# Moving transposes of k with q to the DMA queue from chunk 8, of x from chunk 12, in a new program order

## The chip, the cores and the metric

One core of a Trainium2 chip. The metric is the device time of the program in microseconds (us); most executions agree within a per cent, and a median of several is quoted. All comparisons are with runs of the kernel before in the same session. The sessions of the experiments were on different chips (2, 12, 0, 14 and 7), and the median of the kernel before moved from 186.6 to 187.6 us between sessions, so ratios are worth more here than medians. A ratio is the mean time of one kernel's fast runs over the mean of the other's fast runs of the same rounds, so it is not quite the ratio of the medians beside it.

## The reference

A gated linear recurrence over 4 batches x 8 heads x 768 steps, head size 48, whose output is the input of an MLP with the gate h cos(h):

```python
for t in range(S):
    state = alpha[:, :, t, :, None] * state + einsum('bhd,bhe->bhde', k[:, :, t], v[:, :, t])
    y[:, :, t] = einsum('bhd,bhde->bhe', q[:, :, t], state)
x = y.transpose(0, 2, 1, 3).reshape(3072, 384)
h = x @ w_in                      # 384 -> 2048
out = (h * cos(h)) @ w_out        # 2048 -> 384
```

The kernel cuts the 3072 tokens into 24 chunks of 128. Within a chunk the recurrence is turned into matrix products: scores of scaled q with scaled k, masked, times v, plus q times the state so far.

## The kernel before

Every chunk needs its scaled k and q (the tile `kqb`) transposed for the scores, and its output y transposed into x for the MLP. Each transpose exists in two forms, chosen by the chunk's number: eight (or three) matmuls against the identity on TensorE into a PSUM bank plus a copy by VectorE, or one transposing DMA that SyncE issues.

```python
TD = 13
QB = 6
XD = 13
...
def transposes(j):
    ...
    if j >= TD:
        t = work.tile([C, 2 * NP, C], BF, tag="qkT", bufs=QB)
        nc.sync.dma_start_transpose(out=t, in_=kqb[:, j % 3].rearrange("s i h d -> s (i h d)"))
        qkT_t[j] = t.rearrange("r b s -> r (b s)")
        return
    t = ps.tile([C, 2 * NP * C], BF, tag="g")
    ...     # eight nc.tensor.transpose; ev_transposes() copies the bank out on VectorE

def x_transposes(j):
    if j >= XD:
        x = work.tile([C, 3, C], BF, tag="xT", bufs=3)
        nc.sync.dma_start_transpose(out=x, in_=y_t.pop(j))
        ...
```

All loads of alpha, k, q, v and the weights are DMAs that SyncE issues too, one after the other in program order; ScalarE issues the stores of the result and a small copy of the decays. The order of all work is a hand-written string of units, each a letter and a chunk (or a pair of chunks):

```python
ORDER = ("a0 l0 C0 a2 l1 k0 C1 q0 E0 K0 E1 Q0 w8 T0 t0 v0 k2 N0 ...")
# a k q v: loads;  l C E: decays (log, sums, exps);  K Q b: GpSimd scales k, q, casts v
# T t: transposes of kqb and their copy;  A m: scores, mask;  S u: state;  Y y: outputs and their copy
# D B: transposes of x and their copy;  F G: first MLP product, two halves;  f_ g_ p Q_: gate
# V W: second MLP product, two halves;  e: result out;  w: warm-up matmuls
```

In the traces each engine works through its part of this order in turn, a unit that waits holds the later ones of its engine, and a DMA that waits for its input on SyncE holds the loads behind it. In the kernel before, SyncE had come to the next two transposes of x at 135.7 us; it issued them at 137.7 and 140.9, each when VectorE's copy of its y had ended, and the load of k behind them at 142.3.

## Time and profile before

| | before |
|---|---|
| median time, first session | 186.19 us (186.08 to 189.03) |
| span of the profiled execution | 185.2 us |
| TensorE busy | 173.1 us, 93% |
| first MLP matmul / end of the last one | 26.11 / 181.72 us |
| stops of TensorE in between | 2.4 us |
| transposing DMAs of kqb / of x | 11 / 11 |

A stop is counted from the starts of successive matmuls: where the distance exceeds the usual one of that kind of matmul by over 0.15 us, the excess is a stop. What remains between the first MLP matmul and the end of the last one is called work below. The first line below, from the page of the kernel before, is the mean busy share of the 16 DMA engines in tenths, in 40 slices of 4.6 us; the second is the queue of SyncE's DMAs, with packets, MB and the share of the engines' time:

```profile
DMA  6999999999999999998999889985994964222012
q1 hardware_dynamic: 108304, 29.14, 76.5%
```

Until about 125 us, the DMA engines are as full as TensorE is.

### The profile page before, as it was taken

Reading aid. Unit: us, or ns where it says so; the run is one execution under the profiler, and the core shown is the slowest. Engines: PE = TensorE matmul, PEld = TensorE weight load, DVE = VectorE, ACT = ScalarE, POOL = GpSimd, SP = SyncE. Lnnn points to the kernel's source line nnn. Section 1 sums busy time; section 2 is a strip of 40 time slices with the busy share of each in tenths; the row PEclk is TensorE's granted clock in tenths of the full one; section 3 lists DMA queues with packets and bytes.
Section 4 is the critical chain, followed back from the end, with each engine's and each line's share of the span. In section 5 each row is a group of like instructions: output and inputs, shape, how many; then the busy total and the mean of one; then the engine's idle time right before and its main releaser. Section 6 shows DMA issues by size and latency. Waiting matters only on the chain.

```text
span 185.2 us, 5549 instructions
## 1 busy us (share of the span) xinstructions
PE 173.1 (93%) x2326; PEld 135.7 (73%) x2329; DVE 132.1 (71%) x183; ACT 121.4 (66%) x140; POOL 75.8 (41%) x106
## 2 busy tenths in 40 slices
PE   0898888999999999999989999999999999999992
PEld 0555567986688878779848798698767989698761
DVE  6477799999677875986793897916792877655620
ACT  3855589698568679779578777776468726353521
POOL 3373730419345472927942812684032753100000
PEclk9999999999999999999999999999999999999999
DMA  6999999999999999998999889985994964222012
GB/s 147 261 261 229 360 386 333 373 187 211 211 226 157 237 188 204 198 213 166 221 146 250 165 150 191 198 186 100 188 183 89 203 146 103 64 66 65 4 42 85
DMA packets 113080, 34.24 MB, mean 185 GB/s; under 512 B 106400, under 2 KB 111520, under 8 KB 113056
## 3 DMA queue, kind: packets, MB, share of 16 engines
q1 hardware_dynamic: 108304, 29.14, 76.5%
q10 hardware_dynamic: 4752, 4.76, 8.1%
q8 instruction: 18, 0.29, 0.7%
q14 instruction: 6, 0.05, 0.1%
HBM read 25.17 MB, written 4.72 MB: 161 GB/s over the span
## 4 chain that ended last, share of the span: by engine, by line
PE 83%; DVE 8%; DMA 5%; ACT 1%; issue 1%; DVEq 0%
PE o_new L488 33%; PE t L466 32%; DMA t<-kqb 3%; PE t L371 3%; DVE t L380 3%; PE t L428 2%; DMA a_new<-in_alpha_dram 2%; PE t L396 2%; DVE t L357 2%; PE w_new L504 2%; PE cum_new L227 2%; PE t L344 2%; PE t L425 2%; PE t L449 1%; DVE w L160 1%; PE t L315 1%
## 5 line engine op out<-in xcount | busy, mean ns | idle before, releaser
L466 PE MATMUL t<-x,w 128*128 128x128 bf16 x1152 | 70.3, 219 | 0.0
L488 PE MATMUL o_new<-w,g_new 128*128 128x384 bf16 x384 | 68.0, 326 | 0.0
L480 DVE TENSOR_TENSOR g_new<-t,c_sb 128x1024 bf16<-128x1024 f32 x48 | 57.6, 1218 | 13.0 <-ACT c_sb L474 12.9
L466 PEld LDWEIGHTS <-w 128*128 128x128 bf16 x1152 | 65.7, 98 | 1.1
L474 ACT ACTIVATE c_sb<-t,halfpi 128x1024 bf16<-128x1024 f32 x48 | 52.7, 1112 | 21.1 <-PE t L466 18.9
L488 PEld LDWEIGHTS <-g_new 128*128 128x128 bf16 x384 | 35.6, 98 | 20.9
L380 DVE TENSOR_TENSOR t<-t,mask_f 128x1024 bf16<-128x1024 f32 x24 | 29.0, 1218 | 2.2 <-PE t L371 2.2
L410 POOL TENSOR_TENSOR ub<-sc,Em 128x384 bf16<-128x384 f32 x16 | 13.3, 829 | 36.2 <-DVE sc L408 35.9
L279 POOL TENSOR_TENSOR kqb<-raw_new,cpx 128x384 bf16<-128x384 f32 x18 | 21.3, 1188 | 15.4 <-DMA raw_new<-in_q_dram 9.1
L493 ACT ACTIVATE o_sb<-o_new 128x384 f32<-128x384 f32 x24 | 11.7, 488 | 18.0 <-PE o_new L488 18.0
L263 POOL TENSOR_TENSOR kqb<-raw_new,icp_new 128x384 bf16<-128x384 f32 x18 | 18.0, 1001 | 5.3 <-DMA raw_new<-in_k_dram 3.9
L435 DVE CAST t<-t 128x384 bf16<-128x384 f32 x24 | 13.3, 553 | 7.5 <-PE t L428 7.4
L288 POOL CAST vpb<-raw_new 128x384 bf16<-128x384 f32 x20 | 9.9, 504 | 14.0 <-DMA raw_new<-in_v_dram 6.5
L408 DVE TENSOR_TENSOR sc<-t,ub 128x384 f32<-128x384 f32 x16 | 8.9, 554 | 7.3 <-PE t L396 7.2
L238 ACT ACTIVATE icp_new<-cum_new 128x768 f32<-128x768 f32 x12 | 9.7, 809 | 5.5 <-PE cum_new L227 3.4
L474 ACT ACT_TABLE_LOAD x8 | 10.3, 1283 | 2.9 <-DVE t L435 0.6
L183 ACT ACT_TABLE_LOAD x8 | 10.3, 1283 | 2.0 <-ACT o_sb L493 1.2
L428 PE MATMUL t<-vpb,t 128*128 128x48 bf16 x192 | 11.3, 183 | 0.3 <-DVE t L357 0.3
L428 PEld LDWEIGHTS <-t 128*128 128x128 bf16 x192 | 9.6, 96 | 1.1 <-DVE t L357 0.6
L425 PE MATMUL t<-ub,t 128*128 128x96 bf16 x80 | 9.7, 204 | 0.4 <-DVE t L357 0.4
L371 PE MATMUL t<-t 48*128 48x128 bf16 x192 | 8.2, 218 | 0.7 <-DMA t<-kqb 0.7
L357 DVE COPY t<-t 128x512 bf16<-128x512 bf16 x12 | 7.7, 684 | 1.2 <-PE t L331 1.2
(68 smaller groups left out, 146.6 us busy)
## 6 DMA issues: line engine op xcount, KB each, us to landing
out_dram<-o_sb ACTq DMA_DIRECT2D x24, 192.0 KB, 3.1
raw_new<-in_v_dram SPq DMA_DIRECT2D x20, 192.0 KB, 4.7
a_new<-in_alpha_dram SPq DMA_DIRECT2D x18, 192.0 KB, 4.9
raw_new<-in_k_dram SPq DMA_DIRECT2D x18, 192.0 KB, 4.5
raw_new<-in_q_dram SPq DMA_DIRECT2D x18, 192.0 KB, 4.7
wf<-in_moe_w_in_dram SPq DMA_DIRECT2D x4, 768.0 KB, 8.8
wf<-in_moe_w_out_dram SPq DMA_DIRECT2D x4, 768.0 KB, 9.7
a_new<-in_alpha_dram SPq DMA_DIRECT2D x3, 384.0 KB, 4.6
```

The source lines that it names most:

```text
L263: nc.gpsimd.tensor_tensor(out=khb[:, j % 3, :, 0:D], in0=k_t.pop(j), in1=icp.rearrange("s (h d) -> s h d", h=H), op=ALU.mult)
L279: eng.tensor_tensor(out=qhb[:, j % 3, :, 0:D].rearrange("s (p a) d -> s p a d", a=2), in0=q_t.pop(j).rearrange("s (p a) d -> s p a d", a=2 ...
L371: nc.tensor.matmul(t[:, ACOL[h] * C : (ACOL[h] + 1) * C], qkT_t[j][base : base + D, p * C : (p + 1) * C], qkT_t[j][base : base + D, (NP + ...
L380: nc.vector.tensor_tensor(out=t.rearrange("s (h t) -> s h t", h=H), in0=A_ps.pop(j).rearrange("s (h t) -> s h t", h=H), in1=mask_f.unsquee ...
L410: eng.tensor_tensor(out=ub[:, us(j), :, 0:96].rearrange("r p (a e) -> r p a e", a=2), in0=sc.rearrange("r p (a e) -> r p a e", a=2), in1=E ...
L425: nc.tensor.matmul(t[:, p * 96 : (p + 1) * 96], qT[:, (NP + p) * C : (NP + p + 1) * C], ub[:, us(j - 1), p], start=True, stop=False, skip_ ...
L428: nc.tensor.matmul(t[:, h * D : (h + 1) * D], A_t[j][:, ACOL[h] * C : (ACOL[h] + 1) * C], vpb[:, j % 3, h], start=first, stop=True, skip_g ...
L435: nc.vector.tensor_copy(out=t, in_=y_ps.pop(j)[:, 0:HD])
L466: nc.tensor.matmul(t[:, f], w1[:, kk, ft * C : (ft + 1) * C], x_t[j][:, kk], start=(kk == 0), stop=(kk == 2))
L474: nc.scalar.activation(out=c_sb, in_=h_ps[j, half], func=AF.Sin, bias=halfpi, scale=1.0)
L480: nc.vector.tensor_tensor(out=g_new, in0=h_ps.pop((j, half)), in1=c_t.pop((j, half)), op=ALU.mult)
L488: nc.tensor.matmul(o_ps[j][:, 0:DM], g[:, f], w2[:, half * HF + f], start=(f == 0 and half == 0), stop=(f == HF - 1 and half == 1))
```

## The change

Intent: TensorE is the bound, so take five chunks' transposes of k with q, and one of x, off it and off VectorE, and put them on DMA, in an order meant to suit.

```diff
-    TD = 13
+    TD = 8
     QB = 6
-    XD = 13
+    XD = 12
     ...
     ORDER = (
-        "a0 l0 C0 a2 l1 k0 C1 q0 E0 K0 E1 Q0 w8 T0 t0 v0 k2 N0 b0 n0 N1 n1 v2 M0 M1 T1 t1 o0 w5 S0 o1 E_0 a4 "
+        "a0 k0 l0 C0 E0 a2 K0 w13 T0 l1 N0 q0 Q0 t0 v0 C1 q2 b0 M0 n0 E_0 o0 k2 a4 E1 K2 T1 t1 w6 S0 u0 A0 l2 "
     ...  # the whole string is new; nothing else is
```

## The prediction

> **What bounds the kernel now.** I read the page's busy shares first, then the chain of work that ended last, then TensorE's instructions in order of time, the costliest groups, and last the DMA issues.
>
> ```profile
> PE 173.1 (93%) x2326; PEld 135.7 (73%) x2329; DVE 132.1 (71%) x183; ACT 121.4 (66%) x140; POOL 75.8 (41%) x106
> ...
> PE   0898888999999999999989999999999999999992
> ...
> PE 83%; DVE 8%; DMA 5%; ACT 1%; issue 1%; DVEq 0%
> ```
>
> The page's chain has its shares by engine in that last line. From the costliest groups (mean ns of one after the busy time, then idle time before it), what the change removes:
>
> ```profile
> L360 DVE COPY t<-t 128x1024 bf16<-128x1024 bf16 x7 | 4.8, 689 | 3.5 <-PE t L344 3.4
> L454 DVE COPY x<-t 128x384 bf16<-128x384 bf16 x13 | 4.6, 352 | 2.7 <-PE t L449 2.7
> ...
> L449 PE MATMUL t<-ident_bf,t 128*128 128x128 bf16 x39 | 4.3, 220 | 0.6 <-DVE t L435 0.5
> L344 PE MATMUL t<-ident_bf,kqb 128*128 128x128 bf16 x56 | 4.3, 219 | 0.0
> ```
>
> TensorE is nearly always occupied, no other engine passes 71%, and 83% of the chain lies on TensorE. A mean of 219 ns for a transpose is not its cost, because matmuls overlap. The chain in order of time gives the cost, the time that a unit adds:
>
> ```profile
> 34.40 0.17 PE t L449 x3
> 34.56 2.68 PE t L466 x48
> ...
> 45.33 0.45 PE t L344 x8
> ...
> 89.69 6.04 DMA t<-kqb
> ...
> 176.52 5.21 PE o_new L488 x32
> 181.76 0.49 ACT o_sb L493
> ```
>
> So half a chunk's first MLP product (24 matmuls) costs 1.34 us, half of the second (8) 1.30, a chunk's transposes of k with q (8) 0.45, its transposes of x (3) 0.17. The last matmul ends at 181.76 of a 185.2 us span; the 3.5 us after it are one copy and one store. The MLP alone is 48 x 1.34 + 48 x 1.30 = 126.7 us.
>
> TensorE's instructions in order of time, and ScalarE's casts of the weights, show where it still stops:
>
> ```profile
> 23.26 0.63 ACT L158 ACTIVATE w<-wf 128x512 bf16<-128x512 f32 x1 [1.86 <-DMA wf<-in_moe_w_in_dram]
> ```
>
> ```profile
> 26.11 1.50 PE L466 MATMUL t<-x,w 128*128 128x128 bf16 x24
> ...
> 28.64 0.34 PE L449 MATMUL t<-ident_bf,t 128*128 128x128 bf16 x3 [0.32 <-DVE t L435]
> ...
> 32.52 0.20 PE L425 MATMUL t<-ub,t 128*128 128x96 bf16 x1 [0.42 <-DVE t L357]
> ...
> 95.77 0.40 PE L371 MATMUL t<-t 48*128 48x128 bf16 x8 [0.69 <-DMA t<-kqb]
> ```
>
> Three stages follow. Up to 26.1 us nothing of the MLP runs: its weights are still on the way (the first quarter of the first matrix lands at 23.24 us, the second at 25.27, each 2.03 us apart in a stream with no gap). From 26.1 to 33 us TensorE works with stops. After that it is full, except for 0.69 us at 95 us. From the first MLP matmul to the last one are 181.76 - 26.11 = 155.65 us. From the pitch of successive matmuls against each kind's usual pitch I count stops of 0.45, 0.58, 0.28, 0.17 and 0.76 us, together 2.24 us; the other 153.4 us are work.
>
> [...] The trace [...] shows 219 ns a transpose, of which only 56 ns keep TensorE: it is the smaller number that a removed transpose is worth. [...] Two of them issued one behind the other land 0.75 us apart here (99.17 and 99.92 us), 256 KB in 0.75 us or 350 GB/s[...]; but issue to landing is 3.6 us in the median and 6.0 at worst, since they stand behind loads. [...] I add up pitches and not the 93%.
>
> **The change part by part.**
>
> Transposes of k with q: chunks 8 to 12 go from TensorE to DMA (16 chunks in place of 11). TensorE loses 5 x 0.45 = 2.25 us. VectorE loses 5 copies of 0.69 = 3.4 us. DMA gains 5 x about 0.9 us.
>
> Transposes of x: chunk 12 alone. TensorE loses 0.17 us, VectorE 0.35, DMA gains some 0.4 (the distance of two such landings, 117.11 and 117.53).
>
> Order, before the first MLP matmul: the same twelve loads stand ahead of the weights in both programs, so I expect the first two quarters at about 23.2 and 25.3 us again. The new program starts on the first half of the MLP, of which the quarter that is loaded second is needed first: 25.3 plus a cast of 0.6 gives 25.95 to 26.05 us. No gain here, though VectorE's work ahead of it now leaves more gaps: the start is bound by DMA.
>
> Order, after it: the same MLP units, scores, outputs and states; one permutation (0.33 us) now lies before the first MLP matmul, two warm-up matmuls (2 x 0.217) lie after it. The work from the first MLP matmul on is 153.4 - 2.25 - 0.17 - 0.33 + 0.43 = 151.1 us.
>
> ScalarE: counting the switches between logarithm and sine in program order gives 14 table loads, not 16: 2 x 1.28 = 2.6 us less on an engine with a third of its time idle; worth nothing by itself.
>
> Stops: the transposes, states, outputs and x share one PSUM bank (tag g, one buffer), so each must be copied out before the next may start. Summing TensorE's durations between neighbours in the order, against the copy that has to fit in between, I find two places that don't fit in the program before (0.38 and 0.05 us short, the first where the 0.45 us stop is) and none in the new one, which also has six users of that bank fewer. The 0.45, 0.28 and most of the 0.58 should go.
>
> New stops: in the last three chunks the order leaves 4.8, 4.1 and 3.9 us of other TensorE work between an output's matmuls and the first use of its transposed x, where it left 10.4, 5.7 and 5.3 us. What must fit is a copy (0.55) and a transpose DMA (2.3 / 3.1 / 4.3 us minimum, median, maximum): 2.9 to 4.9 us. At the median it fits, at the worst it is 1 us short each. I allow 0.5 us there, 0.5 for transposes behind loads around chunks 8 to 18 (the scores of chunks 8, 9 and 16 to 18 stand right behind their transposes in the order, though SyncE may issue these earlier), and 0.5 for the start from 26 to 42 us, where weights land one after another up to 39.6 us and the new order consumes them just behind. Together 1.5 us.
>
> Sum: 26.0 + 151.1 + 1.5 = 178.6 us for the last matmul, plus 3.5 = 182.1 us of span, 3.1 below 185.2. In times: 186.2 - 3.1, about 183.1 us.
>
> **The rivals.**
>
> One: the transposes on DMA turn into waits. For it: the only long stop past 33 us is one (0.69 us), it ends a 6.04 us flight, and SyncE issues loads and transposes in one order, so a transpose that waits for k or q holds back all loads behind it. Chunks 8 to 12 fall where loads still stream (loads land about every 1.0 us until 92 us). Against it: ten of eleven such transposes made TensorE wait for nothing, and GpSimd, which makes their inputs, is busy 41%. If every one of the five cost 0.7 us, 3.5 us would be lost: about 185.6 to 186.6 us.
>
> Two: the order has removed more than I see. If the stops shrink to 0.5 us in all, and the start gains half a microsecond because loads are arranged better, the span is 25.5 + 151.1 + 0.5 + 3.5 = 180.6 us, a time of 181.6.
>
> Three: the relief of VectorE and ScalarE is what counts. Against it: VectorE is 71% busy, ends few of TensorE's waits after 33 us, and its longest waits are for ScalarE and TensorE. Then only TensorE's 2.3 us would be gained by accident; a kernel with the old order and the new limits would tell.
>
> **Range and chances.** TensorE's own sum, -2.3 us, is sure to some 0.3 us. The stops may be 0.5 to 4 us (2.2 now), the start 25.5 to 26.8 us. So 183.1 us, with 181.4 to 185.3 for eight in ten. Faster by over 2% is below 182.5 us; that needs stops under 0.9 us, which I give 0.32. Within 2%: 0.65. Slower by over 2% would need over 7 us of waits: 0.03.
>
> **What would show it.** In the new profile: 16 transposes of kqb on TensorE (chunks 6 and 7; the group of L344 falls from x56 to x16) and 16 transpose DMAs of kqb, 12 of x; the first MLP matmul at 26 us, behind a weight's cast; stops of TensorE after it of about 1.5 us; the last matmul at 178 to 179 us with one copy and one store after it. I would be wrong if TensorE showed waits for kqb's or x's transposes of over 2 us in sum, if the first MLP matmul moved by over a microsecond, or if the weights of the second MLP product, which land last, hold up its first use at about 38 us.

## The result, and the profile after

The changed kernel took 192.45 us (191.42 to 193.35, 4 runs) against 186.64 us (186.08 to 189.03): ratio 1.032, 95% interval 1.024 to 1.040. It is slower. The 189.03 us of the kernel before, over 1.5% above its fastest run, is not in the ratio.

From its page: busy time, TensorE's row, the DMA engines' row, and the shares of the chain by engine.

```profile
PE 174.1 (91%) x2289; PEld 133.6 (70%) x2293; DVE 129.6 (68%) x177; ACT 118.4 (62%) x138; POOL 76.8 (40%) x106
...
PE   0899999999999999977989999999999879996992
...
DMA  6999999999897999999959999999998997121102
...
PE 48%; DMA 20%; SPq 11%; DVE 8%; POOL 6%; issue 3%; ACT 2%; ACTq 0%; POOLq 0%
```

The chain that was 83% TensorE is now 48% TensorE; 31% of it are DMAs and SyncE's issuing of them. TensorE's row has a dip at 81 to 91 us, with a small one at 96, and two near 153 and 172 us. TensorE's instructions in order of time show the five long stops (in brackets the idle time of the engine and what ended it):

```profile
82.62 0.34 PE L396 MATMUL t<-vpb,kqb 128*128 128x96 bf16 x4 [1.43 <-POOL kqb L263]
...
89.64 1.50 PE L466 MATMUL t<-x,w 128*128 128x128 bf16 x24 [1.22 <-ACT cpx L245]
...
96.60 1.47 PE L488 MATMUL o_new<-w,g_new 128*128 128x384 bf16 x8 [1.10 <-DVE g_new L480]
...
154.48 1.74 PE L466 MATMUL t<-x,w 128*128 128x128 bf16 x28 [1.94 <-DMA x<-t]
...
174.41 1.51 PE L466 MATMUL t<-x,w 128*128 128x128 bf16 x24 [1.74 <-DMA x<-t]
```

None of the five ends with a transposed kqb. The first waits for GpSimd's scaled k of chunk 12, the second and third for ScalarE and VectorE, the last two for x of chunks 19 and 22. Counted by the distances of matmuls they are 1.59, 1.37, 1.27, 2.10 and 1.90 us, together 8.2 of 10.0 us of stops. The same sum as in the prediction:

| us | before | predicted | after |
|---|---|---|---|
| first MLP matmul | 26.11 | 26.0 | 26.87 |
| work | 153.25 | 151.1 | 151.24 |
| stops | 2.36 | 1.5 | 10.01 |
| copy and store at the end | 3.5 | 3.5 | 3.4 |
| span | 185.2 | 182.1 | 191.6 |

(The prediction counted 2.24 us of stops and 153.4 us of work before.) The saving on TensorE is there to 0.15 us. Of the 9.5 us between the predicted and the measured span, 8.5 are stops. What GpSimd, ScalarE and VectorE were themselves waiting for is told by the chain of waits of the changed kernel, in order of time:

```profile
72.20 5.74 DMA raw_new<-in_q_dram
...
79.02 1.19 POOL kqb L279
80.21 0.95 POOL kqb L263
...
83.36 0.49 SPq L337
...
87.02 5.35 DMA raw_new<-in_q_dram
...
95.31 1.24 DVE g_new L480
96.60 1.47 PE o_new L488 x8
```

A load of q lands late; GpSimd scales q and k late; a transposing DMA that waits on SyncE (L337) is issued late, the loads behind it too; the next load of q lands late. So the first cause lies in the loads. In the summary of waits, GpSimd's waits for loaded q doubled (total, times, longest); first the kernel before, then the changed one:

```profile
POOL kqb L279 <- DMA raw_new<-in_q_dram: 9.1, 3, 7.7
```

```profile
POOL kqb L279 <- DMA raw_new<-in_q_dram: 18.2, 8, 5.3
```

### The profile page after: what moved, and what is told of

It reads as the page before. It is cut to its first block, busy times and chain, and to the rows that moved or that the text cites.

```text
span 191.6 us, 5452 instructions
## 1 busy us (share of the span) xinstructions
PE 174.1 (91%) x2289; PEld 133.6 (70%) x2293; DVE 129.6 (68%) x177; ACT 118.4 (62%) x138; POOL 76.8 (40%) x106
## 4 chain that ended last, share of the span: by engine, by line
PE 48%; DMA 20%; SPq 11%; DVE 8%; POOL 6%; issue 3%; ACT 2%; ACTq 0%; POOLq 0%
PE t L466 17%; PE o_new L488 17%; DMA raw_new<-in_q_dram 9%; SPq L146 8%; DMA x<-t 5%; PE w_new L504 3%; POOL kqb L263 3%; DVE g_new L480 2%; POOL kqb L279 2%; DMA raw_new<-in_v_dram 2%; PE t L371 2%; DMA a_new<-in_alpha_dram 2%; DMA raw_new<-in_k_dram 2%; DVE t L435 1%; PE t L428 1%
## 5 line engine op out<-in xcount | busy, mean ns | idle before, releaser
L466 PE MATMUL t<-x,w 128*128 128x128 bf16 x1152 | 71.1, 219 | 4.9 <-DMA x<-t 3.7
L410 POOL TENSOR_TENSOR ub<-sc,Em 128x384 bf16<-128x384 f32 x16 | 13.9, 871 | 47.8 <-DVE sc L408 47.8
L197 ACT ACTIVATE lnab<-a_new 128x768 bf16<-128x768 f32 x9 | 7.6, 844 | 3.2 <-DMA a_new<-in_alpha_dram 3.2
L504 PE MATMUL w_new<-warm 128*128 128x512 bf16 x29 | 9.1, 444 | 0.2
```

What stands on the lines that cost most here:

```text
L410: eng.tensor_tensor(out=ub[:, us(j), :, 0:96].rearrange("r p (a e) -> r p a e", a=2), in0=sc.rearrange("r p (a e) -> r p a e", a=2), in1=E ...
L466: nc.tensor.matmul(t[:, f], w1[:, kk, ft * C : (ft + 1) * C], x_t[j][:, kk], start=(kk == 0), stop=(kk == 2))
L504: nc.tensor.matmul(w_ps, warm[:, 0:C], warm, start=True, stop=True)
```

## The experiments

The theories to tell apart:

- **Stream.** The DMA engines are the full resource up to about 100 us, and each of the five transposes takes far more of the stream than its bytes; all loads behind them, and what needs those, come later.
- **Head of line.** A transpose waits on SyncE for GpSimd's k and q, and holds the loads behind it; the transfer itself is cheap.
- **Order.** The new order alone is slower: it leaves too little room for x in the last chunks, and transposes have little to do with it.

### The two parts of the change apart

Only the limits, in the order of the kernel before (copies for the transposes left out where they no longer exist):

```diff
-    TD = 13
+    TD = 8
-    XD = 13
+    XD = 12
```

> The old program order with the new limits alone: transposes of k with q by DMA from chunk 8, of x from chunk 12. Theory L (the DMA stream of chunks 6 to 16 is already full, so five more transposes of 256 KB push every later load back and GpSimd gets q and k late): slower than the kernel before, 188 to 191 us, with stops of TensorE between 75 and 110 us. Theory O (the new order makes the waits, the limits only take 2.4 us off TensorE): 183.5 to 186 us, no stops but those of before.

Measured: 195.45 us (194.12 to 196.75) against 187.02, ratio 1.046 [1.038, 1.054]; result right. So without the new order the limits cost more, not less. The worst place in TensorE's order of time, and the page's row of its granted clock:

```profile
88.03 0.61 PE L371 MATMUL t<-t 48*128 48x128 bf16 x8 [6.79 <-DMA t<-kqb]
```

```profile
PEclk9999999999999999965799999999999999999999
```

The scores of chunk 11 waited 6.8 us for their transposed kqb, which in this order stands on SyncE behind seven loads of k and alpha, most of them of later chunks, and was issued at 83.06 us. After the stop, 46 distances of MLP matmuls were 107 ns in place of 56, from 88.7 to 93.5 us. The row has 6, 5 and 7 tenths in its slices from 81.9 to 96.3 us, the stop among them. So this stop of 6.8 us was charged a second time, through the clock; this inflates the 195 us. The new order is partly a repair of this: in the old one the limits alone lose.

Only the order, with all transposes below chunk 13 on TensorE again, placed as they came:

```diff
-    TD = 8
+    TD = 13
-    XD = 12
+    XD = 13
     # t8 to t12, B12 put back into the order, A behind t
```

> The new program order with the old limits (13 and 13): chunks 8 to 12 transposed by TensorE again, some of these transposes moved by a few places so that the shared PSUM bank does not stop them. Theory L: the stops of 1.3 to 1.6 us between 80 and 96 us go, and only those of the last chunks (some 2 us each at chunks 19 and 22) stay: 186 to 189 us. Theory O: the stops stay where they are, and 2.4 us of TensorE work come on top: 192 to 195 us.

Measured: 192.37 us (191.49 to 194.91, one of four runs slow), 1.029 [1.020, 1.038]; result right. The number lies where Order was expected to put it. But it can't be held against Stream as it stands: several of its stops between 64 and 91 us are TensorE transposes, states and outputs that wait for the one PSUM bank they share (0.32 to 0.65 us before four of the transposes of kqb), and I had placed them close together. It was repeated with better placing, below.

### Is the stream of loads the limit?

The changed kernel without its loads of v from chunk 6 on; old data are used, so the result is wrong:

```diff
-        "v": lambda j: load("v_sb", v, v_t, j), ...
+        "v": lambda j: load("v_sb", v, v_t, j) if j < 6 else stale_v(j), ...
```

> The changed kernel without the loads of v from chunk 6 on (18 loads of 192 KB less; it computes with old data of v, so its result is wrong on purpose). Theory L: the loads of q and k land about 1 us earlier a chunk, the stops between 80 and 96 us vanish, 184 to 188 us. Theory O: the stops come from the order of TensorE's and GpSimd's work, which is the same: 191 to 193 us.

Measured: 185.95 us (184.97 to 187.25, 16 runs), 0.994 [0.991, 0.996]. The stops fell from 10.0 to 2.6 us with nothing else changed: same order, same transposes, same waits of the transposes for k and q. With a stream that is less full, the change costs nothing. This is what Stream asks for, and against Order as the main cause. It does not separate Stream from Head of line, since fewer loads also stand behind the transposes. The kernel before was not run without these loads; its stops were 2.4 us in all, so it had little to gain in stops.

### What do the five transposes cost, and through what?

Three versions of the changed kernel, all wrong: the scores of chunks 8 to 12 read a tile of zeros, so no instruction reads these transposes. In the first they are not there. In the second they are issued as in the changed kernel, from `kqb`. In the third they are issued at the same place from a tile that is always ready, so that they hold up nothing on SyncE.

```diff
+        if TD <= j < 13:
+            qkT_t[j] = stale          # first: no transpose at all
+            return
```

> The changed kernel with the five transposes of chunks 8 to 12 left out altogether: their scores read a tile of zeros, so the result is wrong on purpose; nothing else moves. If these five are what costs (by load, by the queue's wait or by the wait for their landing), the stops between 80 and 96 us vanish and only those of the last chunks stay: 185 to 187.5 us. If the rest of the new order makes the stops: 190 to 193 us.

```diff
-            qkT_t[j] = t.rearrange("r b s -> r (b s)")
+            qkT_t[j] = stale if j < 13 else t.rearrange("r b s -> r (b s)")     # second
```

> The same, but the five transposes are issued as in the changed kernel, behind k and q, and nobody reads what they write (scores read the tile of zeros; wrong on purpose). If the cost is TensorE's wait for their landing: like the kernel without them, 185 to 187.5 us. If it is their load on the DMA stream or the queue standing still behind k and q: 189.5 to 192.5 us.

```diff
-            nc.sync.dma_start_transpose(out=t, in_=kqb[:, j % 3]...)
+            nc.sync.dma_start_transpose(out=t, in_=(kqe[:, 0, 0] if j < 13 else kqb[:, j % 3])...)   # third
```

> The same as the unwaited one, but the five transposes read a tile that is always ready, so the queue never stands still for k or q. If plain load on the DMA stream costs: 189 to 192 us, near the unwaited one. If the queue's wait for k and q costs: 185 to 187.5 us, near the one without transposes.

| version | median us | ratio to before [95%] | stops, us |
|---|---|---|---|
| none | 187.37 (14 runs) | 0.997 [0.994, 1.000] | 3.6 |
| issued, nobody reads | 192.59 | 1.024 [1.019, 1.030] | 7.9 |
| issued from a ready tile, nobody reads | 191.77 | 1.020 [1.014, 1.027] | 8.6 |
| the changed kernel | 192.45 | 1.032 [1.024, 1.040] | 10.0 |

The five transposes cost 2.3% (1.020 less 0.997) of 187.4 us, 4.4 us, where they wait for no input and no instruction reads them. Taking k and q as their source adds 0.4% (0.8 us), within the intervals; having them read adds less than 1%, also within them. So Head of line and TensorE's own waits for kqb are small terms, and the cost comes with the transfers themselves. One wait for them is left even here, through a shared semaphore; it is shown further below.

The same five unread transposes were put into the kernel before, as additions in the old order. A first build of this with five new buffers didn't fit into SBUF (the last pool wanted 26.5 KB per partition, and 25.7 were left) and never ran:

> The kernel before with all its TensorE transposes, plus five DMA transposes of 128x1024 bf16 from a tile that is always ready into a spare one, placed where chunks 8 to 12 are transposed. It adds only load to the DMA stream, no wait for k or q. Theory L in its strong form (bandwidth alone): 188 to 190 us. If the wait of the queue for k and q (head of line) is what delays the loads, or under theory O: 186 to 187 us, like before.

With four buffers in turn:

```diff
+    def extra(j):
+        nc.sync.dma_start_transpose(out=spare[:, j % 4], in_=kqe[:, 0, 0].rearrange("s i h d -> s (i h d)"))
     # x8 to x12 in the order, each ahead of its T
```

> The kernel before with all its TensorE transposes, plus five DMA transposes of 128x1024 bf16 from a tile that is always ready into four spare ones that nobody reads, placed where chunks 8 to 12 are transposed (an earlier build of it had no room for five). If the DMA stream of the old order is as full as that of the new one: 4 to 5 us more, 190.5 to 192 us. If the old order keeps a reserve in which 4.5 us of stream time are hidden: 186.5 to 188.5 us.

Measured: 195.84 us (193.72 to 196.52), 1.043 [1.034, 1.051], result right. Five DMAs that nobody reads cost the tuned kernel 8 us. One line of TensorE's order of time says how:

```profile
93.54 0.48 PE L401 MATMUL t<-vpb,kqb 128*128 128x96 bf16 x4 [3.71 <-POOL vpb L288]
```

TensorE waits for GpSimd, which waits for a load of v. The stop was followed by 2.3 us at the slow distance of 107 ns, and an earlier one of 1.9 us, at 81 us, by eight matmuls of the second MLP product at 320 ns in place of 162. The page's clock row has 6 tenths from 82.4 to 87.3 and from 92.1 to 97.0 us. So part of the 8 us is again the clock.

### Bytes, or transposes?

256 KB more in a full stream may cost something whatever moves them. The last of this series replaces the five unread transposes by plain copies of the same bytes, from the same tile to the same buffers, at the same place:

```diff
-            nc.sync.dma_start_transpose(out=t, in_=(kqe[:, 0, 0] if j < 13 else ...))
+            if j < 13:
+                nc.sync.dma_start(out=t.rearrange("r b s -> r (b s)"), in_=kqe[:, 0, 0]...)
```

> The changed kernel in which each of the five DMA transposes of chunks 8 to 12 is replaced by a plain DMA copy of the same 256 KB from the same always-ready SBUF tile into the same buffer, at the same place of the queue, and the scores of these chunks read a zero tile. Wrong on purpose. It is to be held against the version with nothing in that place (187.4 us, 0.997 of the kernel before) and the version with transposes there that nobody reads (191.8 us, 1.020). Theory one, the cost is that of a transpose: until it is complete on every engine the next load does not start. A plain copy of the same bytes shares the stream with its neighbours: 187.5 to 189.5 us, 0.998 to 1.01, and the landing after a copy is put off by 0.7 us or less instead of 1.85. Theory two, the cost is that of 256 KB more in a full stream, whatever moves it: 191 to 192.5 us, 1.018 to 1.025, with each following load put off by 1.3 us or more.

Measured: 187.86 us (186.82 to 190.48, 22 runs), 1.0035 [1.0015, 1.0055], in another session than the three versions above. The copies cost 0.6% (1.0035 less 0.997), 1.2 us; the transposes, 4.4. Landing times of the load ahead of the first two transposes and of the load behind them, and the same around the last three:

| landed, us | none | copies | transposes from a ready tile | changed kernel |
|---|---|---|---|---|
| v of chunk 9, then k of chunk 10 | 62.73, 63.63 | 62.83, 65.35 | 63.06, 67.79 | 63.03, 68.17 |
| distance | 0.90 | 2.52 | 4.73 | 5.14 |
| alpha of chunk 17, then q of chunk 13 | 77.49, 79.64 | 80.82, 83.97 | 81.42, 88.16 | 81.81, 88.49 |
| distance | 2.15 | 3.15 | 6.74 | 6.68 |

Less about 1.0 us for the load itself, a copy took 0.7 us of the stream (1.5 for two, 2.2 for three) and a transpose 1.9 (3.7 for two, 5.7 for three). Held against the 2.15 us of the version with none, the three add 1.0 and 4.6. Where the difference lies can be seen in the DMA view of a few microseconds, cut into 40 slices of 0.1 us: the mean busy share of the engines (a packet's time is counted where it starts), what they moved, and the queue of instruction fetches (packets, MB, share of one window). First the version with transposes from a ready tile, from 63 to 67 us:

```profile
DMA  9999999399999980000000000001999999999999
GB/s 292 287 262 292 287 292 253 56 430 271 253 238 107 18 2 0 0 0 0 3 8 8 10 8 10 10 10 26 230 255 267 255 267 159 207 205 179 187 190 184
...
q8 instruction: 1, 0.02, 1.7%
```

Then the version with copies, from 62.5 to 66.5 us:

```profile
DMA  9999999999999999999999789999999966532200
GB/s 403 328 323 419 293 283 294 338 296 273 269 270 256 255 257 246 229 215 360 171 133 131 106 113 188 204 204 221 225 219 215 148 88 81 75 48 40 40 10 15
...
q8 instruction: 1, 0.02, 2.0%
```

In the first, the engines move nearly nothing from 64.3 to 65.7 us although issued loads are queued. In the trace's packets, 25 pieces of 256 bytes or less that started between 64.20 and 64.45 us (19 of a transpose, four completions, two of a load) all end at 65.8. A fetch of 16 KB runs from 63.90 to 65.00; from 64.9 to 65.75 single packets of the transpose follow one another, and then everything moves again. One late engine, busy with the fetch, would look like this, but that it was so is not shown: the packed trace doesn't name a packet's engine. In the second there is such a fetch too, and no gap. The changed kernel shows the same gap at 64.4 to 65.9 us, and both have another of 1.2 us at 84.5 us.

The packets of all 18 kept traces show when this happens. Call it a freeze when six or more packets under 8 KB that start during a fetch of 16 KB, or up to 0.6 us after it, take over 0.6 us each. After 26 us there are 306 such fetches. Beside 70 of them at least 200 packets of a transpose started, and 53 of these fetches came with a freeze (with any such packet, 63 of 129; 1.2 us in the median); beside 177 no packet of a transpose started, and none came with one. So what froze the stream was mostly a transpose that met an instruction fetch. It is not a rule for each transpose that the loads behind it wait until it is complete on every engine: in the kernel before, 1385 packets of loads, all issued behind a transpose, started from 111.03 to 112.61 us while the last of its sixteen completions was missing. Of the 9.4 us that the five transposes took above, two freezes, of 1.6 and 1.2 us, are 2.8. They are not the whole: in a later version (tail3, below) no fetch met the five, nothing froze from 58 to 92 us, and the two distances of the table were still 5.12 and 6.10 us. Why the two get in each other's way was not tested, and no run moved the fetches.

Both of my theories for this run got a part of their numbers right. By the time, and by the distances around the transfers, the cost is that of a transpose. But the load of k of chunk 15 landed at 87.76, 94.16 and 97.76 us (none, copies, transposes): the copies delayed it by 6.4 us, 1.3 each, and still cost only 1.2 us of time. So some 6 us of lateness at that point are slack. Nine traces that have the new order up to 100 us agree on this (tail3, tail_slack, tail2 and x_on_pe are versions described below):

| version | k of chunk 15 landed, us | stops of TensorE from 75 to 100 us |
|---|---|---|
| none | 87.76 | 0 |
| copies | 94.16 | 0.6 |
| tail3 | 94.72 | 1.0 |
| tail_slack | 96.05 | 2.4 |
| tail2 | 97.21 | 4.1 |
| transposes from a ready tile | 97.76 | 4.5 |
| changed kernel | 98.14 | 4.7 |
| transposes issued, nobody reads | 98.19 | 4.4 |
| x_on_pe | 98.41 | 5.0 |

In tail3 all five transposes are there and are read, and the stops are still 1.0 us in place of 4.7. Its trace is that of the fastest of its six runs: k of chunk 15 landed 3.4 us earlier than in the changed kernel, of which 1.5 were there before the first of the five. Where the copies lose more than the 3.7 us counted around them, I did not trace.

One more wait came with the late landings. All 154 DMAs of the changed kernel share eight completion semaphores, 19 or 20 on each, and in these traces a DMA was not issued before the earlier one on its semaphore had landed. ScalarE's instructions in order of time in the changed kernel:

```profile
87.50 0.48 ACTq L249 DMA_DIRECT2D tot<-cpx  x1
88.08 0.81 ACT L238 ACTIVATE icp_new<-cum_new 128x768 f32<-128x768 f32 x1 [3.01 <-PE o_new L488]
...
92.45 0.34 ACTq L494 DMA_DIRECT2D out_dram<-o_sb  x1
92.87 1.28 ACT L474 ACT_TABLE_LOAD   x1 [2.18 <-DMA raw_new<-in_q_dram]
```

The first issue was held for 2.4 us until the transpose of chunk 12 landed at 87.42, the second for 1.7 us until q of chunk 15 landed at 92.37; neither uses these data. All of ScalarE stood behind them, and TensorE's stops at 88 and 95 us follow. In the kernel before, the longest such hold of ScalarE was 0.26 us. The version with transposes from a ready tile has the same wait, so it is not true that nothing waits there: ScalarE's copy of the decays was held 2.7 us until the fifth transpose landed at 87.45, and TensorE's stop of 1.8 us follows:

```profile
87.52 0.54 ACTq L251 DMA_DIRECT2D tot<-cpx  x1
```

```profile
89.73 1.50 PE L468 MATMUL t<-x,w 128*128 128x128 bf16 x24 [1.62 <-ACT cpx L247]
```

With copies this hold was 0.9 us, behind a load of q. How the 4.4 us divide between late loads and this semaphore no run tells.

### What the order costs by itself

The version with none of the five transposes has 2.0 us less work on TensorE than the kernel before (151.3 for 153.25), and is 0.3% or 0.5 us faster. So the order loses about 1.5 us. The two long stops left in it, in TensorE's order of time, are for x:

```profile
148.20 2.85 PE L471 MATMUL t<-x,w 128*128 128x128 bf16 x48 [1.22 <-DMA x<-t]
...
167.74 1.46 PE L471 MATMUL t<-x,w 128*128 128x128 bf16 x23 [1.34 <-DMA x<-t]
```

The x of chunk 19 was issued behind loads of q and v; that of chunk 22 met a fetch. Its DMA view in the changed kernel, 169.1 to 174.5 us:

```profile
DMA  0000000003999999610500000000000000001899
```

Fifteen of its sixteen completion signals were there by 172.08 us, the last at 174.36; a 16 KB fetch ran from 171.74 to 172.88; on which engine is not shown.

All x transposes on TensorE instead:

```diff
-    XD = 12
+    XD = 24
     # D12 to D23 moved and B12 to B23 added in the order
```

> The changed kernel with all transposes of x on TensorE (12 more, 2.0 us of TensorE work), each put a unit or two earlier in the order; transposes of k with q by DMA from chunk 8 as before. If the two stops of 1.7 and 1.9 us at chunks 19 and 22 are x's transposes landing late: they vanish, and so does a part of the other waits (12 DMAs less): 188 to 191 us. If they only move elsewhere: 192 to 195 us.

Measured: 198.27 us, 1.056 [1.053, 1.060], result right. A miss as a repair: the two stops for x went, but others came (2.3 us at 111 us, before a sum of decays; 1.5 us at 158 us, where a state waits for x to be copied out of the PSUM bank that both now use); stops in all 13.9 us.

Two moves of late units in the changed kernel (outputs of chunks 19 and 23 one MLP unit earlier):

```diff
-  e15 V16 W16 a23 l11 C11 u19 e16 E11 D18 m19 m20 Y19 y19
+  e15 V16 u19 m19 m20 Y19 y19 W16 a23 l11 C11 e16 E11 D18
-  u22 G22 Y23 g_22 y23 F22 Q_21 V21 W21 f_22 e21 D23 Q_22 F23
+  u22 Y23 y23 D23 V21 G22 g_22 Q_21 F22 f_22 W21 e21 Q_22 F23
```

> The changed kernel; only the last chunks' order is moved: the outputs of chunk 19 stand one half product earlier, those of chunk 23 ahead of an MLP half of chunk 22, which is moved back behind a half product of chunk 21. This gives x of chunks 19, 22 and 23 1.4 to 1.7 us more between its making and its use. If the stops of 1.4 to 1.9 us before the MLP of chunks 19 and 22 are x's transposes landing late for want of slack: both go, 188.5 to 190 us. If what holds there is the delayed stream of loads behind: 191 to 193 us.

Measured: 190.34 us (189.65 to 192.44), 1.018 [1.010, 1.025], result right: 1.4% less than the changed kernel, though the stop before chunk 19 (1.6 us) was still there.

The order alone again, with the TensorE transposes spread out so that a copy fits between each two users of the bank, and then with these two moves as well:

> The new order with the old limits (13 and 13), chunks 8 to 12 transposed by TensorE with at least one half product around each of the transposes, so that the shared PSUM bank does not stop them as it did in the first such run. Compared with the run without any transposes for these chunks (187.4): 2.4 us of TensorE work more. If the DMA load of the five was the whole cost: 188.5 to 190.5 us, the two late stops for x still there. If the new order has other waits: over 191 us.

> The same with the last chunks' order moved as in the tail run. If the two causes (load of five transposes; x late at chunks 19 and 22) add up and explain the whole loss: 186 to 188 us, level with the kernel before. If something else is in the new order: 189 us or more.

Measured: 191.12 us (190.88 to 193.65), 1.023 [1.016, 1.031], and 193.75 us (192.18 to 194.04), 1.032 [1.027, 1.038]; both right. Both lie in the ranges given for other waits in the new order. Work 153.4 us in both, as expected for transposes on TensorE; stops 7.8 and 8.2 us, in more than ten places of up to 1.4 us. The second is a plain miss, since 186 to 188 us had been expected: the stop for x of chunk 19 went (1.4 us), and one of the same size appeared at 144 us, where the state of a chunk waits for VectorE. These two runs show that the old form of the transposes does not fit into this order as I placed it. They do not give the price of the order.

Two last pairs of runs asked it directly, on the version with no transposes in chunks 8 to 12 and on the whole changed kernel. In the first pair, x of chunks 18 to 21 went ahead of the loads that stood before it in the queue:

```diff
-  e15 V16 W16 a23 l11 C11 u19 e16 E11 D18 m19 m20 Y19 y19 G18 k22 q21 Y20 F18 v21 q22 v22 ... D19
+  e15 V16 u19 m19 m20 Y19 y19 D18 D19 W16 a23 l11 C11 e16 E11 G18 k22 q21 Y20 F18 v21 q22 v22
   # D20 and D21 moved up likewise, outputs of chunk 23 as in the moves above
```

> The version with no transposes at all in chunks 8 to 12 (wrong on purpose, 187.4 us, 0.997), with the x transposes of chunks 18 to 21 moved ahead of the loads in the queue that stood before them, and the outputs of chunks 19 and 23 moved up by one or two MLP units. If what the new order costs is the wait for the x transposes of chunks 19 and 22 (1.4 and 1.5 us of stops), they go, TensorE's stops fall from 3.6 to 1 to 2 us, and the time is 184.5 to 186 us, 0.982 to 0.99. If the waits only move elsewhere, or the order loses its time in another place: 187 us or more, 0.995 or above.

> The whole changed kernel (192.4 us, 1.03) with the same edit of the last chunks; its result is right. If the x waits are a cost beside that of the five transposes: the stops at 152 and 172 us (2.1 and 1.9 us) go and the time is 188 to 189.5 us, 1.003 to 1.012, still not faster than the kernel before. If the late stops only take in slack that was lost earlier: 191 us or more.

Measured: 194.78 us, 1.040 [1.036, 1.043], and 199.68 us (196.02 to 201.82, result right; five of six runs were classed slow, so there is no ratio). My edit was at fault: D19 waited 5.6 us on SyncE for the copy of the outputs and held the load a23, on which the decays depend, and TensorE stood. In the order of time and in the page's clock row of the first of the two:

```profile
147.49 0.80 PE L229 MATMUL cum_new<-lnab,triu_bf 128*128 128x384 bf16 x2 [5.12 <-ACT lnab L199]
148.08 2.76 PE L471 MATMUL t<-x,w 128*128 128x128 bf16 x24
```

```profile
PEclk9999999999999999999999999999995699999999
```

The 24 MLP matmuls after the stop took 2.76 us, where the prediction's chain has 1.34 for half a chunk. The trace has 56 ns between matmuls of this size elsewhere and 107 for 4.4 us after this stop, and the row above has 5 and 6 tenths from 144.8 to 154.5 us. A much shorter stop was once followed by the same, the one of 1.9 us at 81 us above. The "slow" class of tail2 is probably this too, and no other state of the chip: its trace has a stop of 5.2 us at 151 us and the slow distance after it, its clock row has 5 and 8 tenths from 148.4 to 158.2 us, and the kernel before ran fast beside it.

In the second pair, only three loads (v21, q22, v22) were moved behind D19, and the outputs of chunk 23 up:

```diff
-  G18 k22 q21 Y20 F18 v21 q22 v22 ... f_18 D19 p18
+  G18 k22 q21 D19 Y20 F18 v21 q22 v22 ... f_18 p18
```

> No transposes in chunks 8 to 12 (wrong on purpose; 187.4 us, 0.997 in the changed order), with three loads moved behind the x transpose of chunk 19 in the queue, and the outputs of chunk 23 one MLP unit earlier. If the two stops for x (1.4 us at chunk 19, 1.5 us at chunk 22) are what the order costs: chunk 19 gains about 1 us (its transpose then flies 2 to 3 us, not 5.6), chunk 22 0.5 to 1.5; 185 to 186.3 us, 0.987 to 0.993. If the order loses elsewhere: 187 us or more, 0.995 or above.

> The changed kernel (192.4 us, 1.03), result right, with the same edit. If the x waits add to the cost of the five transposes: 189 to 191 us, 1.01 to 1.02, about 2 us less than the changed kernel, and not faster than the kernel before. If they only take up slack: 192 us or more.

Measured: 187.54 us (186.18 to 189.28), 0.999 [0.996, 1.002], and 191.30 us (188.71 to 192.26), 1.022 [1.017, 1.027], the latter with the right result. Both stops for x went. In their place, in the second kernel's order of time:

```profile
155.11 0.40 PE L371 MATMUL t<-t 48*128 48x128 bf16 x8 [1.88 <-DMA t<-kqb]
```

The loads that now come later delay q and k of chunk 21, and with it the transposed kqb. In this part of the order a wait that is removed comes back two units later. What the new order costs by itself is therefore measured (about 1.5 us, from the version with none of the transposes) and seen as waits for late transfers around 150 and 170 us, but no edit of mine removed it, and whether one could stays open. No correct version beat the kernel before; 190.3 us is the best correct one with the new limits.

## Why the prediction was wrong

**TensorE's saving: right.** "The work from the first MLP matmul on" was predicted at 151.1 us and measured at 151.24. The group of transposes of kqb fell to 16, as said.

**The start: nearly right.** 26.87 us for 26.0.

**"DMA gains 5 x about 0.9 us": this step failed.** The 0.9 us was my estimate. It is near the distance of two transposing DMAs of kqb that landed 0.75 us apart, one behind the other (at 99.17 and 99.92 us). For the packets alone the size is not far off: from 63.0 to 63.5 us of the view above, with nothing else moving, some 110 of a transpose's 1024 packets started every 0.1 us. But it is not what a load behind a transpose pays: from a ready tile, the five took 1.9 us each of the stream, the two freezes included, where a plain copy took 0.7. And the figure was entered in no sum, as if the time lay beside other work. The row that shows the engines full until 125 us was on the page and was not used for it. The term should have been 5 x 1.9 = 9.5 us on a resource with some 6 us of slack; it cost 4.4 us with no instruction reading the transposes.

**New stops, "together 1.5 us": measured 10.0.** The 0.5 us for transposes behind loads looked for the loss at TensorE's waits for kqb, and there it is in fact small (the longest, before the scores at 66.6 us, is 0.41 us). It appeared where the *loads* are used: 1.59 us for the scaled k of chunk 12, and 1.37 and 1.27 us through ScalarE, held by the completion of transfers it does not need. The 0.5 us for the start came nearly as said (0.36 and 0.16 us up to 33 us). The 0.5 us for x in the last chunks was right in kind and too small: 2.10 and 1.90 us. "At the worst it is 1 us short each" took the longest flight seen before, 4.3 us; in the changed kernel, flights of 5.3 and 5.2 us did the harm. And chunk 19, where the first of them fell, was not among the chunks I had listed as tight.

**The rivals.** Rival one, transposes turn into waits, was nearest. It argued that transposes would hold loads, but priced this at 0.7 us each and for the wrong reason, the wait for k and q on SyncE: transposes that wait for nothing cost nearly as much (1.020 against 1.024). Rival three was asked by running only the limits, and fell by 195 us. Rival two had no support: the order removed the old small stops and brought others.

**The chances.** 0.03 for slower by over 2%: "would need over 7 us of waits". By the prediction's own sum the limit is 8.3 us of stops (its 1.5, and the 6.8 us from 183.1 to 189.9), not 7; 10.0 came. The chance ignored that a second resource was full.

## What to carry to other kernels

Before moving work to DMA, read the row of the DMA engines in the stages where it will land. If that row is full, price the move by how much later the next load lands and not by the transfer's rate, and ask who uses those loads. Expect a transposing DMA among loads to cost well over its bytes (here 1.9 us of the stream, and 0.7 for a plain copy of the same 256 KB), look for instruction fetches that meet it (here 53 of 70 such fetches came with a freeze; all the freezes took 1.2 us in the median), keep it where the stream has gaps (without the loads of v from chunk 6 on the whole change cost nothing, 0.994), and keep long stops away from TensorE: past the first MLP matmul, those of 2.7 us and over, up to 6.8, were all followed here by 2 to 5 us with 107 ns between MLP matmuls in place of 56, and so was one of 1.9 us by matmuls of the second MLP product at 320 ns in place of 162; the others under 2.7 were not.
